# Casting k and q of the first pair inside the set-up, with its products in the score banks and one load moved to another queue

## The chip, the cores and the metric

The kernel runs on one core of one Trainium2 chip. The metric is device microseconds (us) for one execution, measured on the chip. Each timed set also has one profiled execution. In every execution the listed time is about 1.7 us longer than the span that the profile covers, so a span of 435.3 us belongs to a time of 437.0 us.

Engines are named as in the profile: PE is TensorE, PEld its weight loads, DVE is VectorE, ACT is ScalarE, POOL is GpSimd, SP is SyncE.

## The reference

Two stages follow each other. The first is causal attention with a decay that comes from a running sum of log(f). The second is a spectral mix: a Fourier transform along the sequence, one complex 512 x 512 matrix for each of 64 modes, the inverse transform, and a channel product.

```python
# batch 8, heads 8, seq 576, head_dim 64; 64 modes, d_model 512
scores = (q @ k.T) / sqrt(64) + (cum[:, None] - cum[None, :])   # cum = cumsum(log f), causal
attn   = softmax(scores);  x = attn @ v          # heads side by side: [8, 576, 512]
X = rfft(x, axis=1)[:, :64]                      # Xr, Xi
Yr = einsum('bmd,mde->bme', Xr, w_r) - einsum('bmd,mde->bme', Xi, w_i)
Yi = einsum('bmd,mde->bme', Xr, w_i) + einsum('bmd,mde->bme', Xi, w_r)
u  = x + irfft(Y, n=576);  out = u + relu(u @ w_ch)
```

The mode matrices w_r and w_i are 64 x 512 x 512 numbers of 4 bytes each, 134 MB together. They are read once and cast to bf16 on the way in.

## The kernel before

The attention runs in 32 steps. A step is one head of one pair of batches; two steps share one "pair" of loads (k, q, v). Weights are loaded into a ring of 9 tiles, and a tile comes free when the mode products that read it are done. All loads but f and the v of pair 0 are issued by GpSimd in program order.

```python
def emit_loads(pr):                       # k, q, v of one pair
    for nm, src in (("k", k), ("q", q), ("v", v)):
        ...
        if nm == "v" and pr < 1:
            nc.sync.dma_start(dst, ap)    # SP's queue
        else:
            pool_dma(dst, ap)             # GpSimd's queue, in program order
...
nc.vector.tensor_copy(ident_f[:, :], ident_bf[:, :])
...                                        # sel, memsets
nc.scalar.activation(lf[:], ft[:], ACT.Ln)
nc.vector.tensor_tensor_scan(cum[:], onesS[:], lf[:], 0.0, ALU.mult, ALU.add)
cum_ps = psT.tile([128, NSB, BH], F32, tag="tr", name="cum_ps")   # transpose banks
...                                        # transposes of cum, copies, R_ps, Rb
nc.vector.tensor_tensor(biasA[...], Rb..., cumT..., ALU.subtract)
nc.scalar.activation(wdec[:, :, :], biasA[:, :, :], ACT.Exp)
for r0, n in RG:
    cum9_ps = psT.tile([128, 5, BH], F32, tag="tr", name="cum9_ps")
    ...                                    # transposes, subtractions into bias9
nc.scalar.activation(wdec9[:, :, :, :], bias9[:, :, :, :], ACT.Exp)
...
emit_transposes(0, "kqv")   # cast k, q, v of pair 0, transpose them on PE, copy KT, QT, VT
for s in range(NS + 1):
    pr, h = s // 2, s % 2
    if s == 0:
        emit_loads(STG - 1)
    if h == 1 and pr + STG < NPR:
        emit_loads(pr + STG)
    ...                                    # early weight loads; transposes of pair pr + 1
    emit_scores(s, 0); emit_av(s - 1, [0, 1, 2]); emit_scores(s, 1); emit_scores(s, 2)
    if s > B:                              # from step 5 on
        while nmode < (s - B) * NTH // (NS - B):
            emit_modes(nmode)              # 32 or more products of one weight tile
            nmode += 1
            next_w()                       # the load that takes the freed ring tile
    emit_av(s - 1, [3, 4]); emit_scores(s, 3); emit_vback(s)
    ...                                    # step 2: the Fourier basis; even steps: emit_dft
```

Each engine's order of instructions is settled when the kernel is built, unless an instruction is pinned to its place in the program (`keep_in_program_order`).

The softmax here doesn't subtract the row's maximum and nothing guards it: scores larger than these inputs give would overflow.

Of the kernel before, what the change touches and what calls it, by code (L numbers as in the profile page):

```python
# [8 lines left out]
F32 = mybir.dt.float32  # L9
BF16 = mybir.dt.bfloat16  # L10
I32 = mybir.dt.int32
ALU = mybir.AluOpType
# [9 lines left out]
def kernel(  # L22
# [66 lines left out]

    def pool_dma(dst, src):  # L90
        tc.keep_in_program_order(nc.gpsimd.dma_start(dst, src))  # L91
# [133 lines left out]
    with ExitStack() as actx:  # L225
# [34 lines left out]
        def emit_loads(pr):  # L260
            dc, bp, _ = steps[2 * pr]
            for nm, src in (("k", k), ("q", q), ("v", v)):
# [7 lines left out]
                if nm == "v" and pr < 1:  # L270
                    nc.sync.dma_start(dst, ap)
                else:
                    pool_dma(dst, ap)

# [56 lines left out]
        nc.vector.tensor_copy(ident_f[:, :], ident_bf[:, :])  # L331
        for r, t in enumerate(sel):
            nc.vector.memset(t[:, :], 0.0)
            nc.vector.tensor_copy(
                _strided(t[:, 1:2], [[2, 64]]), _strided(ident_bf[:, r : r + 1], [[2, 64]])
            )
# [12 lines left out]
        nc.vector.tensor_tensor_scan(cum[:], onesS[:], lf[:], 0.0, ALU.mult, ALU.add)  # L349
        cum_ps = psT.tile([128, NSB, BH], F32, tag="tr", name="cum_ps")  # L350
# [8 lines left out]
        for h in range(2):  # L359
            nc.vector.tensor_copy(  # L360
                cum2[:, :, h, :], _strided(cum[:, 0:1], [[1, NR], [NR, RP]])
            )
        cumT = scratch(128, NSB, BH)
        nc.vector.tensor_copy(cumT[:, 0:4, :], cum_ps[:, 0:4, :])
        nc.vector.tensor_copy(cumT[:64, 4, :], cum_ps[:64, 4, :])
        ones_row = scratch(1, 128)
        nc.vector.memset(ones_row[:], 1.0)
        R_ps = psT.tile([128, BH], F32, tag="tr", name="R_ps")
        nc.tensor.matmul(
            R_ps[:],  # L370
# [6 lines left out]
        nc.vector.tensor_copy(Rb[:], R_ps[:])  # L377
        biasA = scratch(128, NSB, BH)
        nc.vector.tensor_tensor(
            biasA[:, 0:4, :],  # L380
            _strided(Rb[:, :], [[0, 4], [1, BH]]),
            cumT[:, 0:4, :],
            ALU.subtract,
        )
        nc.vector.tensor_tensor(
            biasA[:64, 4, :], Rb[:64, :], cumT[:64, 4, :], ALU.subtract
        )
        nc.vector.memset(biasA[64:128, 4, :], 0.0)
# [5 lines left out]
        for r0, n in RG:  # L394
            cum9_ps = psT.tile([128, 5, BH], F32, tag="tr", name="cum9_ps")
# [6 lines left out]
            for h in range(2):  # L402
                hs = slice(h * 64, h * 64 + 64)
                nc.vector.tensor_tensor(
                    bias9[hs, r0 : r0 + n, :, :],
                    _strided(Rb[hs, h : h + 1], [[0, n], [H, B], [2, NDC]]),
                    _strided(
                        cum9_ps[hs, 0, h : h + 1], [[BH, n], [H, B], [2, NDC]]
                    ),
                    ALU.subtract,  # L410
                )
# [59 lines left out]

        QT, vaugs = {}, {}

        def emit_transposes(pr, what):
            dc, bp, _ = steps[2 * pr]
            for which in what:
                st = QKVst[pr % STG][which]
                if which == "q":
                    QT[pr] = qtp.tile([128, 2, S], BF16, tag="QT", name="QTs")
                sb = qkb.tile([128, NR, 2, Dh], BF16, tag="cb", name=which + "b")  # L480
                if which != "v":
                    ins = nc.vector.tensor_copy(
                        sb[:, :, :, :].rearrange("p r b d -> p b r d"), st[:, :, :, :]
                    )
                else:
                    ins = nc.vector.tensor_tensor(
                        sb[:, :, :, :],
                        st[:, :, :, :].rearrange("p b r d -> p r b d"),
# [629 lines left out]
```

## Time and profile before

| | before |
|---|---|
| median of 3 executions | 437.05 us (436.73 to 437.52) |
| profiled execution | 438.35 us, span 436.6 us |
| DMA share, 5 to 391 us | 1.12 to 1.14, but 1.03 at 90 to 94 us |
| first scores' exponential starts | 16.63 us |
| first ring wait of GpSimd ends | 83.34 us, after 11.74 us |
| last group of mode products starts | 401.59 us |

The page of the profile cuts the span into 40 slices of 10.9 us. These three lines are the granted clock of TensorE in tenths of full speed, the busy share of the DMA engines in tenths, and what they moved.

```profile
...
PEclk9997589999867758668668698699999896998997
DMA  8999999999999999999999999999999999994697
GB/s 181 235 235 242 234 235 239 230 193 239 230 219 235 220 229 236 212 236 229 219 236 212 211 211 211 211 211 211 212 211 211 211 211 211 211 211 97 234 365 291
...
```

The transfers are at their limit from the second slice to slice 36, and the clock is at half in parts of slices 4 to 6. The table by stage says the same in numbers. Its columns are the stretch and its length in us, busy time (and instructions) of PE, PEld, DVE, ACT and POOL, then the granted clock, the DMA share and the GB/s.

```profile
...
5.00:81.00 76.00, 60.57 (x693) 41.55 (x694) 58.86 (x164) 51.08 (x76) 26.62 (x42) 0.87 1.14 233
81.00:90.00 9.00, 8.84 (x189) 7.00 (x187) 8.24 (x24) 6.95 (x11) 3.32 (x6) 1.00 1.14 236
90.00:94.00 4.00, 4.00 (x83) 3.35 (x79) 3.18 (x11) 3.46 (x7) 2.00 (x4) 1.00 1.03 169
94.00:275.00 181.00, 145.41 (x2407) 111.14 (x2405) 114.34 (x313) 93.31 (x139) 54.72 (x83) 0.76 1.13 224
275.00:391.00 116.00, 106.00 (x1489) 65.41 (x1502) 48.78 (x105) 46.22 (x80) 32.17 (x46) 0.93 1.12 211
...
```

Only the stretch of 90 to 94 us falls off, with 169 GB/s. GpSimd's timeline of before shows why. Columns: start, length, engine, line, operation, output<-input, count, and in brackets the idle time before it and what ended that.

```profile
...
70.84 0.76 POOL L91 DMA_DIRECT2D wch<-in_moe_w_ch_dram  x1 [0.40 <-DMA stv<-in_v_dram]
83.34 0.62 POOL L91 DMA_DIRECT2D wb<-in_moe_w_r_dram  x1 [11.74 <-PE vp L524]
...
87.91 0.62 POOL L91 DMA_DIRECT2D wb<-in_moe_w_r_dram  x1 [3.34 <-PE ps L552]
...
93.28 0.64 POOL L91 DMA_DIRECT2D wb<-in_moe_w_r_dram  x1 [2.00 <-PE A L186]
...
```

GpSimd stood 11.74 us because no ring tile was free, and the next tile came 4.6 us after the first. In that time the queue ran low. The last lines needed are ScalarE's in the set-up:

```profile
...
10.41 0.47 ACT L389 ACTIVATE wdec<-Yacc 128x320 bf16<-128x320 f32 x1 [4.52 <-DVE Yacc L385]
11.74 0.44 ACT L412 ACTIVATE wdec<-Yacc 128x288 bf16<-128x288 f32 x1 [0.87 <-DVE Yacc L404]
12.94 1.36 ACT L513 COPY KT<-tp 128x640 bf16<-128x640 bf16 x2 [0.76 <-PE tp L500]
16.63 1.94 ACT L559 ACTIVATE E<-ps 128x1024 bf16<-128x1024 f32 x2 [2.32 <-PE ps L552]
```

The cast of k started on VectorE at 11.68 us, KT was copied at 12.94 us, and the first scores' exponential (L559) started at 16.63 us.

### The profile page before, as it was taken

The page shows a single profiled execution, that of the slowest core. Times are in us where ns is not written, and L with a number is a line of the kernel's source. Part 1 is how long each engine was busy: PE and PEld are TensorE (multiplying, and loading weights), DVE is VectorE, ACT ScalarE, POOL GpSimd, SP SyncE. Part 2 cuts the span into 40 slices and gives each one's busy share as a digit, 9 for nine tenths or more (in the row PEclk, how much of TensorE's full clock was granted, in tenths as well). Part 3 has the DMA queues.
Part 4 walks back from the last instruction along what each step waited for, and adds up shares of the span by engine and source line. Part 5 has one row for each costly group of instructions (what it writes and reads, how often), then busy time and mean ns, then how long its engine had stood idle before and what let it go on. Part 6 is the DMA issues. An engine that isn't in the chain of part 4 may idle for free.

```text
span 436.6 us, 12199 instructions
## 1 busy us (share of the span) xinstructions
PE 356.7 (82%) x5247; PEld 244.7 (56%) x5265; DVE 263.0 (60%) x658; ACT 224.9 (52%) x340; POOL 129.3 (30%) x202
## 2 busy tenths in 40 slices
PE   2687799998887976877778796999989778898881
PEld 1454566776666655655656565666565444554440
DVE  5687778878565665555657677333333353653892
ACT  3688378776645436446355373234434342642771
POOL 8333332153233232332333222323223223200600
PEclk9997589999867758668668698699999896998997
DMA  8999999999999999999999999999999999994697
GB/s 181 235 235 242 234 235 239 230 193 239 230 219 235 220 229 236 212 236 229 219 236 212 211 211 211 211 211 211 212 211 211 211 211 211 211 211 97 234 365 291
DMA packets 50981, 97.37 MB, mean 223 GB/s; under 512 B 3792, under 2 KB 12976, under 8 KB 50928
## 3 DMA queue, kind: packets, MB, share of 16 engines
q0 software_dynamic: 46688, 86.16, 100.8%
q1 hardware_dynamic: 3920, 9.91, 6.3%
q8 instruction: 41, 0.67, 0.6%
q10 hardware_dynamic: 320, 0.52, 0.5%
q14 instruction: 12, 0.10, 0.1%
HBM read 163.73 MB, written 9.44 MB: 397 GB/s over the span
## 4 chain that ended last, share of the span: by engine, by line
PE 31%; DMA 30%; ACT 11%; DVE 10%; issue 5%; POOL 0%; DVEq 0%; ACTq 0%; SPq 0%
DMA wb<-in_moe_w_i_dram 27%; ACT E L559 7%; PE pav L597 7%; PE ps L552 6%; PE tp L500 5%; PE A L186 5%; DMA stv<-in_v_dram 3%; PE px L640 2%; DVE QTs L515 2%; PE vp L524 2%; ACT KT L513 2%; DVE XT L654 1%; DVE os L984 1%; PE pz L806 1%; DVE E L574 1%
## 5 line engine op out<-in xcount | busy, mean ns | idle before, releaser
L559 ACT ACTIVATE E<-ps 128x1024 bf16<-128x1024 f32 (+1 forms) x128 | 101.7, 855 | 23.8 <-PE ps L552 14.3
L186 PE MATMUL A<-XT,wb 128*128 128x16 bf16 x1984 | 70.7, 182 | 14.2 <-DMA wb<-in_moe_w_i_dram 9.2
L186 PEld LDWEIGHTS <-wb 128*128 128x128 bf16 x1984 | 63.8, 100 | 28.6 <-issue 11.8
L91 POOL DMA_DIRECT2D wb<-in_moe_w_r_dram x64 | 42.9, 670 | 123.5 <-DMA wb<-in_moe_w_r_dram 20.2
L552 PE MATMUL ps<-QTs,KT 64*128 64x64 bf16 (+4 forms) x384 | 55.3, 313 | 18.5 <-ACT E L559 17.2
L91 POOL DMA_DIRECT2D wb<-in_moe_w_i_dram x64 | 42.4, 663 | 83.4 <-DMA wb<-in_moe_w_i_dram 42.3
L597 PE MATMUL pav<-va,E 128*128 128x65 bf16 (+1 forms) x1088 | 53.4, 206 | 4.0 <-DVE x_all L619 3.5
L597 PEld LDWEIGHTS <-E 128*128 128x128 bf16 (+1 forms) x1088 | 43.8, 111 | 19.7 <-issue 9.5
L574 DVE TENSOR_TENSOR E<-E,trimask 128x256 bf16<-128x256 bf16 (+2 forms) x128 | 37.3, 303 | 19.8 <-ACT E L559 19.7
L517 ACT COPY VT<-tp 128x640 bf16<-128x640 bf16 (+1 forms) x32 | 23.1, 757 | 32.4 <-PE tp L500 32.3
L845 ACT CAST XW<-pxw 128x512 bf16<-128x512 f32 x36 | 20.7, 587 | 36.7 <-PE pxw L838 31.8
L888 ACT CAST XW<-pB 128x512 bf16<-128x512 f32 x36 | 20.9, 586 | 31.7 <-PE pB L806 26.3
L552 PEld LDWEIGHTS <-KT 64*128 64x128 bf16 x384 | 18.9, 97 | 30.4 <-issue 21.2
L887 DVE CAST x_all<-pA 128x512 bf16<-128x512 f32 x36 | 24.9, 692 | 17.1 <-PE pA L806 15.3
L838 PE MATMUL pxw<-wch,yy 128*128 128x512 bf16 x133 | 33.7, 386 | 1.1 <-issue 0.5
L513 ACT COPY KT<-tp 128x640 bf16<-128x640 bf16 (+1 forms) x32 | 22.1, 754 | 22.1 <-PE tp L500 22.1
L515 DVE COPY QTs<-tp 128x640 bf16<-128x640 bf16 (+1 forms) x32 | 23.3, 768 | 14.3 <-PE tp L500 14.2
L619 DVE TENSOR_TENSOR x_all<-pav,rcp 128x384 bf16<-128x384 f32 x64 | 29.1, 455 | 0.8
L151 DVE TENSOR_TENSOR YTe<-A,Yacc 128x128 bf16<-128x128 f32 x16 | 5.9, 366 | 33.2 <-PE A L186 33.2
L608 DVE RECIPROCAL rcp<-pav 128x6 f32<-128x6 f32 x64 | 12.1, 190 | 21.4 <-PE pav L597 20.7
L806 PEld LDWEIGHTS <-ident_bf 64*64 64x64 bf16 (+1 forms) x300 | 14.4, 110 | 17.1 <-issue 9.7
L500 PE MATMUL tp<-ident_bf,qb 128*128 128x128 bf16 x144 | 17.4, 276 | 4.6 <-ACT KT L513 3.9
(143 smaller groups left out, 607.9 us busy)
## 6 DMA issues: line engine op xcount, KB each, us to landing
wb<-in_moe_w_r_dram POOLq DMA_DIRECT2D x62, 512.0 KB, 16.9
wb<-in_moe_w_i_dram POOLq DMA_DIRECT2D x62, 512.0 KB, 17.8
stv<-in_v_dram POOLq DMA_DIRECT2D x10, 576.0 KB, 15.2
out_dram<-os SPq DMA_DIRECT2D x10, 512.0 KB, 5.5
stk<-in_k_dram POOLq DMA_DIRECT2D x11, 288.0 KB, 15.3
stq<-in_q_dram POOLq DMA_DIRECT2D x11, 288.0 KB, 15.3
wx<-in_v_dram POOLq DMA_DIRECT2D x5, 576.0 KB, 15.1
out_dram<-uo SPq DMA_DIRECT2D x3, 512.0 KB, 3.9
```

The source lines that it names most:

```text
L91: tc.keep_in_program_order(nc.gpsimd.dma_start(dst, src))
L186: nc.tensor.matmul(A[:, eb, mi, :], lhsT=w_of(mi, eb * 128), rhs=x_of(m), start=(i == 0), stop=(i == len(terms) - 1),)
L500: nc.tensor.transpose(tp[:, r - r0, :, :].rearrange("c h p -> c (h p)"), sb[:, r, :, :].rearrange("p b d -> p (b d)"), ident_bf[:, :],)
L513: nc.scalar.copy(rows(KTs[pr % 2][:, :, 0:S]), tv)
L515: nc.vector.tensor_copy(rows(QT[pr][:, :, :]), tv)
L552: nc.tensor.matmul(ps[:, b, o : o + n], lhsT=KTs[pr % 2][bs, h, jb * 128 : (jb + 1) * 128], rhs=QT[pr][bs, h, jb * 128 + c0 : jb * 128 + c ...
L559: nc.scalar.activation(E[:, :, piece * 512 : piece * 512 + w], ps[:, :, 0:w], ACT.Exp, scale=scale,)
L574: nc.vector.tensor_tensor(dg, dg, tr, ALU.mult)
L597: nc.tensor.matmul(pav[64 * half : 64 * half + w, slot, :], lhsT=E[:, b, c : c + (w - 1) * st + 1 : st], rhs=va[:, jb, b, :], start=(n == ...
L619: nc.vector.tensor_tensor(xo, pi, ri, ALU.mult)
L838: nc.tensor.matmul(pxw[:, :], lhsT=xT[:, eb, i * 128 : (i + 1) * 128], rhs=wch[:, eb, :], start=(eb == 0), stop=(eb == NDC - 1),)
L887: nc.vector.tensor_copy(xs, pA[:, :])
```

## The change

The change brings the first scores forward. The casts of k and q of pair 0 stand amid the set-up, the set-up's products use the score banks, so that the transpose banks are free for k and q, VectorE's order is pinned, and the v of pair 1 goes to SP's queue behind f and the v of pair 0. No arithmetic is added or removed.

```diff
-                if nm == "v" and pr < 1:
+                if nm == "v" and pr < 2:
                     nc.sync.dma_start(dst, ap)
@@ the set-up (keep = tc.keep_in_program_order)
-        nc.vector.tensor_copy(ident_f[:, :], ident_bf[:, :])
-        for r, t in enumerate(sel): ...            # now after emit_transposes(0, "v")
-        nc.vector.tensor_tensor_scan(cum[:], onesS[:], lf[:], 0.0, ALU.mult, ALU.add)
-        cum_ps = psT.tile([128, NSB, BH], F32, tag="tr", name="cum_ps")
+        keep(nc.vector.tensor_tensor_scan(cum[:], onesS[:], lf[:], 0.0, ALU.mult, ALU.add))
+        keep(nc.vector.tensor_copy(ident_f[:, :], ident_bf[:, :]))
+        cum_ps = psS.tile([128, 2, 512], F32, tag="sc", name="cum_ps")
+        cum_ps = cum_ps[:, 0, 0 : NSB * BH].rearrange("p (s c) -> p s c", s=NSB)
 ...                                                # R_ps and cum9_ps likewise to psS
+        emit_transposes(0, "k")
+        keep(nc.vector.tensor_copy(Rb[:], R_ps))
 ...                                                # the biasA subtractions, each kept
+        emit_transposes(0, "q")
         nc.scalar.activation(wdec[:, :, :], biasA[:, :, :], ACT.Exp)
 ...                                                # the bias9 subtractions, each kept
-        emit_transposes(0, "kqv")
+        emit_transposes(0, "v")
```

More of the change, by code (lines that the diff above doesn't have):

```diff
@@ L88, in tile_of @@
         return 2, g ^ 4 if GL // 2 <= g < GL else g
+    keep = tc.keep_in_program_order
     def pool_dma(dst, src):
-        tc.keep_in_program_order(nc.gpsimd.dma_start(dst, src))
+        keep(nc.gpsimd.dma_start(dst, src))
     def wb_tile(n, *dims):
@@ L273, in emit_loads, with emit_transposes, rows @@
                     pool_dma(dst, ap)
+        QT, vaugs = {}, {}
+        def emit_transposes(pr, what):
+            dc, bp, _ = steps[2 * pr]
+            for which in what:
+                st = QKVst[pr % STG][which]
+                if which == "q":
+                    QT[pr] = qtp.tile([128, 2, S], BF16, tag="QT", name="QTs")
+                sb = qkb.tile([128, NR, 2, Dh], BF16, tag="cb", name=which + "b")
+                if which != "v":
+                    ins = nc.vector.tensor_copy(
+                        sb[:, :, :, :].rearrange("p r b d -> p b r d"), st[:, :, :, :]
+                    )
+                else:
+                    ins = nc.vector.tensor_tensor(
+                        sb[:, :, :, :],
+                        st[:, :, :, :].rearrange("p b r d -> p r b d"),
+                        _strided(
+                            wdec9[:, 0, 2 * bp, dc : dc + 1],
+                            [[B * NDC, NR], [NDC, 2], [0, Dh]],
+                        ),
+                        ALU.mult,
+                    )
+                if pr < STG:
+                    tc.keep_in_program_order(ins)
+                for r0, n in RG:
+                    tp = psT.tile([128, 5, 2, RP], BF16, tag="tr", name="tp")
+                    for r in range(r0, r0 + n):
+                        nc.tensor.transpose(
+                            tp[:, r - r0, :, :].rearrange("c h p -> c (h p)"),
+                            sb[:, r, :, :].rearrange("p b d -> p (b d)"),
+                            ident_bf[:, :],
+                        )
+                    tv = tp[:, 0:n, :, :].rearrange("c r h p -> c h p r")
+                    def rows(t):
+                        return t.rearrange("c h (p r) -> c h p r", r=NR)[
+                            :, :, :, r0 : r0 + n
+                        ]
+                    if which == "k":
+                        nc.scalar.copy(rows(KTs[pr % 2][:, :, 0:S]), tv)
+                    elif which == "q":
+                        ins = nc.vector.tensor_copy(rows(QT[pr][:, :, :]), tv)
+                        if pr == 0:
+                            keep(ins)
+                    else:
+                        nc.scalar.copy(rows(VTs[pr % 2][:, :, 0:S]), tv)
         used = [0]
@@ L330 @@
         )
-        nc.vector.tensor_copy(ident_f[:, :], ident_bf[:, :])
-        for r, t in enumerate(sel):
-            nc.vector.memset(t[:, :], 0.0)
-            nc.vector.tensor_copy(
-                _strided(t[:, 1:2], [[2, 64]]), _strided(ident_bf[:, r : r + 1], [[2, 64]])
-            )
         for t in VTs:
@@ L348 @@
         cum = scratch(BH, S)
-        nc.vector.tensor_tensor_scan(cum[:], onesS[:], lf[:], 0.0, ALU.mult, ALU.add)
-        cum_ps = psT.tile([128, NSB, BH], F32, tag="tr", name="cum_ps")
+        keep(
+            nc.vector.tensor_tensor_scan(
+                cum[:], onesS[:], lf[:], 0.0, ALU.mult, ALU.add
+            )
+        )
+        keep(nc.vector.tensor_copy(ident_f[:, :], ident_bf[:, :]))
+        cum_ps = psS.tile([128, 2, 512], F32, tag="sc", name="cum_ps")
+        cum_ps = cum_ps[:, 0, 0 : NSB * BH].rearrange("p (s c) -> p s c", s=NSB)
         for sc in range(NSB):
@@ L359 @@
         for h in range(2):
-            nc.vector.tensor_copy(
-                cum2[:, :, h, :], _strided(cum[:, 0:1], [[1, NR], [NR, RP]])
+            keep(
+                nc.vector.tensor_copy(
+                    cum2[:, :, h, :], _strided(cum[:, 0:1], [[1, NR], [NR, RP]])
+                )
             )
         cumT = scratch(128, NSB, BH)
-        nc.vector.tensor_copy(cumT[:, 0:4, :], cum_ps[:, 0:4, :])
-        nc.vector.tensor_copy(cumT[:64, 4, :], cum_ps[:64, 4, :])
+        keep(nc.vector.tensor_copy(cumT[:, 0:4, :], cum_ps[:, 0:4, :]))
+        keep(nc.vector.tensor_copy(cumT[:64, 4, :], cum_ps[:64, 4, :]))
         ones_row = scratch(1, 128)
-        nc.vector.memset(ones_row[:], 1.0)
-        R_ps = psT.tile([128, BH], F32, tag="tr", name="R_ps")
+        keep(nc.vector.memset(ones_row[:], 1.0))
+        R_ps = psS.tile([128, 2, 512], F32, tag="sc", name="R_ps")[:, 0, 0:BH]
         nc.tensor.matmul(
-            R_ps[:],
+            R_ps,
             lhsT=ones_row[0:1, :],
@@ L376 @@
         Rb = ssb.tile([128, BH], F32, name="Rb")
-        nc.vector.tensor_copy(Rb[:], R_ps[:])
+        emit_transposes(0, "k")
+        keep(nc.vector.tensor_copy(Rb[:], R_ps))
         biasA = scratch(128, NSB, BH)
-        nc.vector.tensor_tensor(
-            biasA[:, 0:4, :],
-            _strided(Rb[:, :], [[0, 4], [1, BH]]),
-            cumT[:, 0:4, :],
-            ALU.subtract,
-        )
-        nc.vector.tensor_tensor(
-            biasA[:64, 4, :], Rb[:64, :], cumT[:64, 4, :], ALU.subtract
-        )
-        nc.vector.memset(biasA[64:128, 4, :], 0.0)
+        keep(
+            nc.vector.tensor_tensor(
+                biasA[:, 0:4, :],
+                _strided(Rb[:, :], [[0, 4], [1, BH]]),
+                cumT[:, 0:4, :],
+                ALU.subtract,
+            )
+        )
+        keep(
+            nc.vector.tensor_tensor(
+                biasA[:64, 4, :], Rb[:64, :], cumT[:64, 4, :], ALU.subtract
+            )
+        )
+        keep(nc.vector.memset(biasA[64:128, 4, :], 0.0))
+        emit_transposes(0, "q")
         nc.scalar.activation(wdec[:, :, :], biasA[:, :, :], ACT.Exp)
@@ L394 @@
         for r0, n in RG:
-            cum9_ps = psT.tile([128, 5, BH], F32, tag="tr", name="cum9_ps")
+            cum9_ps = psS.tile([128, 2, 512], F32, tag="sc", name="cum9_ps")
+            cum9_ps = cum9_ps[:, 0, 0 : 5 * BH].rearrange("p (r c) -> p r c", r=5)
             for r in range(r0, r0 + n):
@@ L403 @@
                 hs = slice(h * 64, h * 64 + 64)
-                nc.vector.tensor_tensor(
-                    bias9[hs, r0 : r0 + n, :, :],
-                    _strided(Rb[hs, h : h + 1], [[0, n], [H, B], [2, NDC]]),
-                    _strided(
-                        cum9_ps[hs, 0, h : h + 1], [[BH, n], [H, B], [2, NDC]]
-                    ),
-                    ALU.subtract,
+                keep(
+                    nc.vector.tensor_tensor(
+                        bias9[hs, r0 : r0 + n, :, :],
+                        _strided(Rb[hs, h : h + 1], [[0, n], [H, B], [2, NDC]]),
+                        _strided(
+                            cum9_ps[hs, 0, h : h + 1], [[BH, n], [H, B], [2, NDC]]
+                        ),
+                        ALU.subtract,
+                    )
                 )
@@ L469, in emit_basis @@
                 )
-        QT, vaugs = {}, {}
-        def emit_transposes(pr, what):
-            dc, bp, _ = steps[2 * pr]
-            for which in what:
-                st = QKVst[pr % STG][which]
-                if which == "q":
-                    QT[pr] = qtp.tile([128, 2, S], BF16, tag="QT", name="QTs")
-                sb = qkb.tile([128, NR, 2, Dh], BF16, tag="cb", name=which + "b")
-                if which != "v":
-                    ins = nc.vector.tensor_copy(
-                        sb[:, :, :, :].rearrange("p r b d -> p b r d"), st[:, :, :, :]
-                    )
-                else:
-                    ins = nc.vector.tensor_tensor(
-                        sb[:, :, :, :],
-                        st[:, :, :, :].rearrange("p b r d -> p r b d"),
-                        _strided(
-                            wdec9[:, 0, 2 * bp, dc : dc + 1],
-                            [[B * NDC, NR], [NDC, 2], [0, Dh]],
-                        ),
-                        ALU.mult,
-                    )
-                if pr < STG:
-                    tc.keep_in_program_order(ins)
-                for r0, n in RG:
-                    tp = psT.tile([128, 5, 2, RP], BF16, tag="tr", name="tp")
-                    for r in range(r0, r0 + n):
-                        nc.tensor.transpose(
-                            tp[:, r - r0, :, :].rearrange("c h p -> c (h p)"),
-                            sb[:, r, :, :].rearrange("p b d -> p (b d)"),
-                            ident_bf[:, :],
-                        )
-                    tv = tp[:, 0:n, :, :].rearrange("c r h p -> c h p r")
-                    def rows(t):
-                        return t.rearrange("c h (p r) -> c h p r", r=NR)[
-                            :, :, :, r0 : r0 + n
-                        ]
-                    if which == "k":
-                        nc.scalar.copy(rows(KTs[pr % 2][:, :, 0:S]), tv)
-                    elif which == "q":
-                        nc.vector.tensor_copy(rows(QT[pr][:, :, :]), tv)
-                    else:
-                        nc.scalar.copy(rows(VTs[pr % 2][:, :, 0:S]), tv)
         def emit_vback(s):
@@ L691, in next_w @@
                 nload += 1
-        emit_transposes(0, "kqv")
+        emit_transposes(0, "v")
+        for r, t in enumerate(sel):
+            nc.vector.memset(t[:, :], 0.0)
+            nc.vector.tensor_copy(
+                _strided(t[:, 1:2], [[2, 64]]), _strided(ident_bf[:, r : r + 1], [[2, 64]])
+            )
         for s in range(NS + 1):
```

## The prediction

> **What bounds it now.** The transfers. The 40-slice strip and the table by stage show DMA busy and flat from 2 us to 391 us: share 1.14 at 5–81 us, 1.13 at 94–275, 1.12 at 275–391 (211 GB/s written for weights cast from f32 to bf16, so about twice that read, an estimate). The Trainium skill, "DMA: Bandwidth & Descriptors" (Anatomy of one DMA), fits a transfer's variable part at 436 GB/s; 2 x 211 = 422 agrees. The chain of waits has 27% of the span on weight transfers, end to end from 275 to 395 us. Then comes a tail of about 42 us of products and output stores, which the change does not touch.
>
> Only three places are not saturated: the start (0–2 us nothing, share 0.89 at 2–5 us); a dip at 90–94 us (169 GB/s, share 1.03, lowest 0.85); the tail. The dip comes from GpSimd's issue list: after 71.6 us it stands 11.7 us because the weight ring is full, until the first mode products end at 83.3 us; the queue then runs nearly dry. Against 210 GB/s the slices of 85–95 us lost about 0.2 MB, worth 0.4 to 1.0 us (an estimate). The chain of waits confirms it: at 70–87 us it runs through ScalarE exponentials and matmuls, then through the weight issues.
>
> **What the change does.** No arithmetic is added or removed.
> - VectorE: the identity cast (0.21 us) moves ahead of the two 1.34 us copies of the sums, so TensorE's transposes of the sums start near 6.2 instead of 7.53 us. The casts of k and q (0.46, 0.45 us) fill waits for the products (0.65 us before the copy at 9.56); the five bias subtractions of the second exponential (0.65 + 0.58 us) go behind the QT copies. QT should end near 12.8 instead of 15.93 us.
> - ScalarE: the KT copies (1.36 us) now come before the Exp table load. That load (1.28 us in the trace; the same 1283 ns in "ScalarE: Activation LUTs", What ACT_TABLE_LOAD costs) was hidden at 4.60 us; now it follows KT, at about 11.3 us. Both decay exponentials precede the first scores' exponential, and the second waits for the bias subtractions, so it starts near 14.5 instead of 16.63 us. vb starts near 14.6 instead of 15.83 us.
> - Set-up products in the score banks free the transpose banks.
> - v of pair 1 moves from GpSimd's queue (0.73 us of issuing) to SP's: same bytes, same 16 engines.
>
> So attention runs 1 to 2 us earlier. Through pair 3 loads lie several us ahead of their casts (pair 2's k lands about 24.5, is cast at 29.1), so the shift should survive to 83 us. There it can only close the dip at 90–94 us. From there the transfers are saturated again, and earlier compute merely waits.
>
> **Prediction.** Gain 0.7 us of the dip, 0 to 0.3 at the start: 436.2 us (range 434.4 to 437.7). Faster by over 2%: 0.02; within 2%: 0.96; slower by over 2%: 0.02.
>
> **What would show it.** First scores' exponential near 14.5 us; GpSimd's long wait ends 1–2 us before 83.3 us; the 90–94 us dip shallower; last weight issue (385.45 us before) and end of transfers 0.5–1 us earlier; 211 GB/s at 275–391 unchanged; tail unchanged.
>
> **What would make it wrong.** TensorE's granted clock drops to 0.50 in stretches (38–58 us); a shift could move one into the tail or the 70–83 us stretch, plus or minus 1–2 us. v of pair 1 beside k and q of pair 0 may delay their landing and eat the shift. If the queue's waits, not bandwidth, set the flat 211 GB/s, more than 1 us could be won.

## The result, and the profile after

Ratios here are the mean time of one kernel's fast executions over that of the other's of the same rounds, so they are not quite the ratio of the medians quoted beside them.

| | before | after |
|---|---|---|
| median | 437.28 us (436.73 to 437.52, 4 executions) | 437.75 us (437.36 to 438.0, 4 executions) |
| ratio | 1 | 1.0012, 95% interval 0.9994 to 1.0029: the same |
| profiled execution | span 436.6 us | span 436.2 us |

The predicted gain of 0.8 us did not come. The median is 0.05 us above the predicted range. The trace of the changed kernel nevertheless shows much of what was expected. The table by stage of after:

```profile
...
5.00:81.00 76.00, 59.35 (x685) 39.35 (x685) 58.78 (x167) 50.72 (x75) 25.51 (x41) 0.91 1.14 232
81.00:90.00 9.00, 8.83 (x165) 6.65 (x164) 6.97 (x18) 6.71 (x10) 2.39 (x4) 1.00 1.15 233
90.00:94.00 4.00, 4.00 (x87) 3.28 (x88) 3.12 (x12) 2.85 (x5) 3.46 (x6) 1.00 1.12 206
94.00:275.00 181.00, 150.28 (x2377) 113.98 (x2375) 114.62 (x315) 94.11 (x141) 54.31 (x81) 0.71 1.13 223
275.00:391.00 116.00, 105.14 (x1501) 65.17 (x1518) 50.07 (x108) 46.39 (x81) 32.14 (x46) 0.93 1.12 211
...
```

The dip at 90 to 94 us is nearly gone, 206 instead of 169 GB/s (a shorter one stands earlier: the slices of 85 to 87 us have 174 and 172 GB/s, in before 185 and 199), and 275 to 391 us is unchanged at 211 GB/s. The set-up on ScalarE in after:

```profile
...
10.74 1.36 ACT L318 COPY KT<-tp 128x640 bf16<-128x640 bf16 x2 [6.37 <-PE tp L305]
12.12 1.28 ACT L448 ACT_TABLE_LOAD   x1
13.42 0.47 ACT L448 ACTIVATE wdec<-Yacc 128x320 bf16<-128x320 f32 x1
15.75 0.44 ACT L474 ACTIVATE wdec<-Yacc 128x288 bf16<-128x288 f32 x1 [1.86 <-DVE Yacc L465]
16.10 2.83 ACT L574 ACTIVATE E<-ps 128x1024 bf16<-128x1024 f32 x3
```

KT is copied at 10.74 instead of 12.94 us, but the first exponential of the scores starts at 16.10 us. The activation table load of 1.28 us (1283 ns in the Trainium skill, "ScalarE: Activation LUTs", What ACT_TABLE_LOAD costs), which was hidden before, is now in the row, and the second decay exponential waits 1.86 us for VectorE. VectorE's timeline of after shows the beginning of that chain:

```profile
...
9.47 0.46 DVE L287 COPY kb<-stk 128x1152 bf16<-128x1152 bf16 x1 [1.52 <-DMA stk<-in_k_dram]
...
11.03 0.46 DVE L287 COPY qb<-stq 128x1152 bf16<-128x1152 bf16 x1 [0.22 <-DMA stq<-in_q_dram]
12.65 1.55 DVE L320 COPY QTs<-tp 128x640 bf16<-128x640 bf16 x2 [1.16 <-PE tp L305]
...
```

The cast of k waited 1.52 us for its own data (stk), and the first copy of QT started at 12.65 us. And GpSimd's first ring wait did not end earlier:

```profile
...
71.64 0.76 POOL L93 DMA_DIRECT2D wch<-in_moe_w_ch_dram  x1 [0.39 <-DMA stv<-in_v_dram]
83.73 0.61 POOL L93 DMA_DIRECT2D wb<-in_moe_w_r_dram  x1 [11.32 <-PE pav L612]
...
88.84 0.61 POOL L93 DMA_DIRECT2D wb<-in_moe_w_r_dram  x1 [3.89 <-PE ps L567]
...
92.18 0.67 POOL L93 DMA_DIRECT2D wb<-in_moe_w_r_dram  x1
...
```

It ended at 83.73 us, against 83.34 us. So of a lead of 0.5 us at the first exponential nothing was left at 83 us. Two traces of one execution each cannot tell which of this belongs to the kernels.

### The profile page after: what moved, and what is told of

The parts are those of the page before. It is cut to its first block, busy times and chain, and to the rows that moved or that the text cites. A ratio compares the mean times of both kernels' runs of the same rounds, so it can differ in the third digit from the quotient of the medians.

```text
span 436.2 us, 12199 instructions
## 1 busy us (share of the span) xinstructions
PE 359.0 (82%) x5247; PEld 245.1 (56%) x5265; DVE 263.1 (60%) x658; ACT 224.9 (52%) x340; POOL 128.2 (29%) x201
## 4 chain that ended last, share of the span: by engine, by line
DMA 40%; PE 28%; ACT 8%; DVE 6%; issue 4%; POOL 1%; DVEq 0%; ACTq 0%; SPq 0%; POOLq 0%
DMA wb<-in_moe_w_i_dram 39%; PE pav L612 7%; PE ps L567 6%; ACT E L574 6%; PE tp L305 5%; PE A L188 5%; DVE QTs L320 2%; ACT KT L318 1%; PE vp L539 1%; DVE os L1004 1%; PE px L655 1%; PE px L680 1%; ACT VT L324 1%; DVE E L589 1%; POOL yy L821 1%
## 5 line engine op out<-in xcount | busy, mean ns | idle before, releaser
L574 ACT ACTIVATE E<-ps 128x1024 bf16<-128x1024 f32 (+1 forms) x128 | 101.4, 849 | 24.8 <-PE ps L567 14.5
L188 PE MATMUL A<-XT,wb 128*128 128x16 bf16 x1984 | 69.5, 181 | 13.2 <-DMA wb<-in_moe_w_i_dram 9.0
L567 PE MATMUL ps<-QTs,KT 64*128 64x64 bf16 (+4 forms) x384 | 59.5, 324 | 20.6 <-ACT E L574 18.6
L612 PE MATMUL pav<-va,E 128*128 128x65 bf16 (+1 forms) x1088 | 55.5, 210 | 2.7 <-DVE x_all L634 2.3
L612 PEld LDWEIGHTS <-E 128*128 128x128 bf16 (+1 forms) x1088 | 45.6, 114 | 18.0 <-issue 9.1
L567 PEld LDWEIGHTS <-KT 64*128 64x128 bf16 x384 | 20.0, 99 | 36.2 <-issue 24.6
L655 PE MATMUL px<-bas,x_all 128*128 128x128 bf16 x160 | 18.8, 270 | 2.4 <-ACT XT L673 1.8
```

Source lines behind the costliest of these rows:

```text
L188: nc.tensor.matmul(A[:, eb, mi, :], lhsT=w_of(mi, eb * 128), rhs=x_of(m), start=(i == 0), stop=(i == len(terms) - 1),)
L567: nc.tensor.matmul(ps[:, b, o : o + n], lhsT=KTs[pr % 2][bs, h, jb * 128 : (jb + 1) * 128], rhs=QT[pr][bs, h, jb * 128 + c0 : jb * 128 + c ...
L574: nc.scalar.activation(E[:, :, piece * 512 : piece * 512 + w], ps[:, :, 0:w], ACT.Exp, scale=scale,)
L612: nc.tensor.matmul(pav[64 * half : 64 * half + w, slot, :], lhsT=E[:, b, c : c + (w - 1) * st + 1 : st], rhs=va[:, jb, b, :], start=(n == ...
```

## The experiments

Theory A: the set-up's time is passed on through the ring wait and the transfers to the end, but less of it arrives than predicted. Theory B: some slack, or the tail, swallows it. Within A, parts of the change may hurt: the v of pair 1 on SP may hold up the k of pair 0 and change the order on the engines. In all there were 18 runs, several of them of the same kernel. "Lead" below is the amount of data landed at 384 us, less that of the first trace of before, summed from tables by stage of 2 us (good to about 0.02 MB). At 211 GB/s, 0.1 MB is 0.47 us.

### Both kernels again, and the load moved alone

before_again is before unchanged, after_again is the changed kernel unchanged. after_vpool undoes one part of the change, before_vsp does that part alone:

```diff
# after_vpool, from after             # before_vsp, from before
-  if nm == "v" and pr < 2:           -  if nm == "v" and pr < 1:
+  if nm == "v" and pr < 1:           +  if nm == "v" and pr < 2:
```

Expected of before_again:

> The kernel before, unchanged, to learn what one trace is worth. Theory 'floor' (transfers set the time; only the dip near 90 us can be won): ratio 1.000 within 0.15%; the new trace again has GpSimd's long wait for a weight ring tile ending at 83.3 plus or minus 0.3 us, and again a stretch of two or more 1 us slices under 190 GB/s between 85 and 95 us. Rival 'noise' (the dip that the prediction counted on is a chance of one execution): the wait ends elsewhere by over 0.5 us, or the dip is absent or half as deep.

Expected of after_again:

> The changed kernel, unchanged, with five rounds to settle the sign. Theory 'floor': ratio 0.998 to 1.001; first scores' exponential at 16.1 us, the long ring wait ends at 83.7, about 0.1 MB more landed than in the kernel before from 94 us on, the last weight lands 0.2 to 0.5 us earlier. Rival 'slower in truth' (the median of 4 runs was 0.5 us up): ratio 1.001 to 1.002 with an interval above 1, and the trace shows a later landing of the last weight or a longer tail.

Expected of after_vpool:

> The changed kernel with v of pair 1 back on GpSimd's queue. Theory 'v on SP ate the lead': k of pair 0 lands before 8.6 us and its cast does not wait (9.47 us and 1.52 us of waiting in the changed kernel), first scores' exponential at 14.3 to 15.0 us; the 64-wide score piece stays ahead of the sine table load, so the lead survives 35 to 43 us and the long ring wait ends at 81.5 to 82.5 us; the dip closes; with 'floor' the ratio is 0.997 to 0.999 (0.4 to 1.2 us). Rival 'set-up on the path one to one': about 2 us faster, 0.995. Rival 'v on SP is harmless': k lands as in the changed kernel and nothing moves.

Expected of before_vsp:

> The kernel before with v of pair 1 on SP alone. Theory 'v on SP ate the lead': k of pair 0 lands after 9.0 us, here without harm since its cast comes at 11.7; GpSimd's issues of pairs 2 and 3 come 0.4 to 0.8 us later; the order near the sine tables changes, and the long ring wait ends 0.5 to 1.5 us later than 83.3. Ratio 0.999 to 1.003. Rival: no change in any of these marks.

Measured, 5 rounds, one chip; the shared executions of before gave 437.48 us (436.61 to 438.89, 11 of them):

| | median us | ratio (95%) | k cast | first exp. | ring wait ends | lead MB |
|---|---|---|---|---|---|---|
| before_again | 437.15 | 0.9995 (0.9975 to 1.0014) | 11.52 | 16.47 | 83.54 | -0.02 |
| after_again | 437.46 | 0.9999 (0.9980 to 1.0019) | 7.93 | 14.98 | 82.52 | +0.20 |
| after_vpool | 437.55 | 0.9997 (0.9978 to 1.0015) | 7.82 | 15.08 | 80.93 | +0.18 |
| before_vsp | 440.87 | 1.0082 (1.0044 to 1.0120) | 11.52 | 16.55 | 85.40 | -0.22 |

The changed kernel's cast of k started at 7.93 us here after a gap of only 0.14 us, so the length of the 1.52 us wait of the first trace was a feature of that execution. In after_vpool the cast did not wait and the ring wait ended earlier, as expected, but the time did not fall to the expected 0.997 to 0.999. The load of v alone made the kernel before 0.8% slower, where 0.999 to 1.003 had been expected. And single executions of one unchanged kernel scatter by more than 2 us, which is more than the whole predicted gain.

### A dose in the bad direction

after_late runs the set-up's scan three times instead of once. The order on VectorE, ScalarE, GpSimd and SP is otherwise that of after.

```diff
-        keep(nc.vector.tensor_tensor_scan(cum[:], onesS[:], lf[:], 0.0, ALU.mult, ALU.add))
+        for _ in range(3):
+            keep(nc.vector.tensor_tensor_scan(cum[:], onesS[:], lf[:], 0.0, ALU.mult, ALU.add))
```

> A dose in the bad direction: the changed kernel with the set-up's scan run three times instead of once on VectorE (the same values written again; no other instruction moves on any engine). One scan is about 1.3 us in the traces, so the first scores' exponential should come about 2.5 us later, at 17.5 to 18.5 us instead of 15.0 to 16.1. Theory A (the set-up time is passed on to the end, and a gain of under 1 us merely drowns in the scatter of single executions): GpSimd's long ring wait ends about 2.5 us later (85 to 86 us), the dip after 84 us is back, at 390 us the transfers are 0.3 to 0.5 MB behind the changed kernel's (1.5 to 2.5 us at 211 GB/s), and the time is 438.7 to 440, ratio to before 1.003 to 1.006. Theory B (slack before the first mode takes up the set-up time): ring wait ends under 1 us later, transfers level, time 437.0 to 437.8, ratio 0.999 to 1.001.

The three scans took 4.12 us. The first exponential came at 17.97 us and the first ring wait ended at 84.93 us, 1.2 to 2.4 us later than in the five traces of the changed kernel. The lead was -0.05 MB, 0.13 to 0.25 MB less than there. The median was 438.52 us beside 438.23 us of before (ratio 1.0017, 0.9989 to 1.0046). The delay is therefore passed on to the ring and to the transfers, as theory A has it, but the ring wait moved by less than 2.7 us and the transfers by less than the expected 0.3 to 0.5 MB. The time alone decides nothing.

### Taking the dip away without touching the set-up

before_modes puts the first two groups of mode products at the end of step 4. after_vm does the same to after_vpool.

```diff
                 if h == 0:
                     emit_dft(pr - 1)
+            if s == B:
+                while nmode < 2:
+                    emit_modes(nmode)
+                    nmode += 1
+                    next_w()
```

> The dip is taken away without touching the set-up: the kernel before, with the first two groups of modes put right after the first transform (at the end of step 4) instead of inside step 5, so that the second ring tile comes free about 3 us earlier. Expected in the trace: the first ring wait ends as in before (about 83.4 us), the second weight tile is issued at about 85 instead of 88 us, the slices from 86 us on are at 200 GB/s or more, at 390 us the transfers are 0.1 to 0.2 MB ahead of before (0.5 to 0.9 us). If the closed dip is worth what the traces say, the median is 436.5 to 437.0 (ratio 0.998 to 0.999); if something after 390 us takes it back, 437.2 to 437.8 although the transfers lead.

> Both together: after_vpool with the first two groups of modes at the end of step 4. If the dip is all that the weights' stream can win, this adds nothing to after_vpool, since no dip is left there (transfers 0.2 MB ahead of before at 390 us, time within 0.3 us of after_vpool2). If freeing the ring earlier wins more than the dip, transfers lead by 0.3 MB or more and the time is 436.2 or less.

Both were slower: before_modes 442.51 us (ratio 1.0115, 1.0090 to 1.0140), after_vm 440.70 us (1.0067, 1.0044 to 1.0090). The edit was badly made. The two weight loads moved ahead of the loads of pair 5 and of wch in GpSimd's order, and GpSimd stood still before them, as its timeline in before_modes shows:

```profile
...
63.46 0.62 POOL L91 DMA_DIRECT2D wb<-in_moe_w_i_dram  x1 [1.82 <-DMA wb<-in_moe_w_r_dram]
82.19 0.61 POOL L91 DMA_DIRECT2D wb<-in_moe_w_r_dram  x1 [18.11 <-PE tp L500]
...
```

It was blocked for 18.11 us, the transfers stopped, and at 384 us the traces were 0.88 and 0.66 MB behind. That is a usable calibration all the same. At 211 GB/s these are 4.2 and 3.1 us, and the mean times were 4.9 and 2.8 us above before. So a lag in the transfers reaches the end nearly whole.

before_modes2 is the repaired edit: the products stand early, the loads stay where they were. after_vm2 is the same edit of after_vpool.

```diff
+            if s == B:
+                for n in range(2):
+                    emit_modes(n)
...
-                    emit_modes(nmode)
+                    if nmode >= 2:
+                        emit_modes(nmode)
                     nmode += 1
                     next_w()
```

> The dip taken away in the kernel before, this time without moving any transfer: the first two groups of modes stand at the end of step 4 as in before_modes, but the loads of weights stay where they were, so that GpSimd issues all transfers in the order of before (before_modes had put two of them ahead of the loads of pair 5, blocked GpSimd from 64 to 82 us and lost 0.88 MB). Expected: second weight tile issued at 85 to 86 us instead of 88, dip gone from 87 us on, at 390 us 0.1 to 0.2 MB ahead of before, and, if a lead is passed on as before_modes and after_vm show a lag to be (0.88 MB and 0.66 MB behind cost 4 and 3 us), a ratio of 0.998 to 0.999 (436.5 to 437.0). If the end takes leads of under 1 us back, 0.9995 to 1.0005.

GpSimd's timeline in before_modes2 shows the second ring tile (84.16 us) right behind the first, where before had 87.91 us:

```profile
...
82.28 0.61 POOL L91 DMA_DIRECT2D wb<-in_moe_w_r_dram  x1 [10.97 <-PE tp L500]
...
84.16 0.61 POOL L91 DMA_DIRECT2D wb<-in_moe_w_r_dram  x1 [0.64 <-PE tp L500]
...
```

No slice of 1 us from 84 to 96 us is under 200 GB/s, and the lead is 0.20 MB, as expected. The profiled execution took 436.37 us, 0.8 us under the mean of before on that chip. But the six executions lay between 436.33 and 439.01 us, median 437.95 us, ratio 1.0013 (0.9993 to 1.0034). The dip can be closed without touching the set-up. What it is worth does not show above the scatter.

### More executions

> The same kernel as after_vpool once more (the changed kernel with the v of pair 1 back on GpSimd's queue), for more executions. The trace should again show no dip (first ring wait ending near 81 us, all slices from 84 us at 190 GB/s or more) and transfers about 0.2 MB ahead of before at 390 us. If that lead is worth its 0.9 us, the median of the fast runs is 436.4 to 436.9; if the lead is lost at the end, 437.2 to 437.7.

> The changed kernel once more, for more executions and one more look at when the k of pair 0 lands. Passed on: half to all of the 0.10 to 0.21 MB lead, ratio to before 0.998 to 0.999. Taken back: 0.9995 to 1.0005. If the landing of k varies with the v of pair 1 ahead of it on the other queue, the cast of k starts anywhere between 7.9 and 9.5 us.

> after_vpool a third time, for more executions: its two looks lead by 0.18 to 0.23 MB at 390 us, its two medians have ratios of 0.9997 and 0.9996. A lead passed on would be 0.998; taken back, 0.9995 to 1.0005.

> The kernel before with the v of pair 1 on SP, once more: its first run was 0.8% slower (437.1 us span in the profile, but 438 to 444 in the other executions), more than the 0.22 MB that its profile was behind explain (1 us). If its cost is real and varies with the execution, the ratio is again 1.005 to 1.012 and this profile shows another depth of the dip after 85 us; if the first run was a fluke of that chip, the ratio is 1.001 to 1.004.

| | median us | ratio (95%) | k cast | ring wait ends | lead MB | span of the trace |
|---|---|---|---|---|---|---|
| after_vpool2 | 437.38 | 0.9996 (0.9970 to 1.0022) | 7.94 | 82.39 | +0.23 | 436.5 |
| after_again2 | 438.01 | 1.0023 (1.0007 to 1.0039) | 8.59 | 82.86 | +0.16 | 434.8 |
| after_vpool3 | 437.26 | 1.0004 (0.9988 to 1.0020) | 7.82 | 80.74 | +0.24 | 436.5 |
| before_vsp2 | 440.28 | 1.0084 (1.0053 to 1.0116) | 11.47 | 86.11 | -0.35 | 438.3 |

The cost of before_vsp is real: two chips gave 1.0082 and 1.0084. In its traces the cast of k and the first exponential stand where before has them (16.55 and 16.42 us), so the landing of k is not the reason there. The ring wait ends at 85.40 and 86.11 us, 2.5 and 3.2 us later than in before on average. The line is from GpSimd's timeline of before_vsp2, with columns as above:

```profile
...
86.11 0.62 POOL L91 DMA_DIRECT2D wb<-in_moe_w_r_dram  x1 [14.45 <-PE vp L524]
...
```

After_vpool, with the same load back on GpSimd's queue, has its ring wait end at 79.9 to 82.4 us in four traces, and its cast of k always at 7.8 to 7.9 us without a wait. The lines are from VectorE's and then GpSimd's timeline of after_vpool3:

```profile
...
7.82 0.38 DVE L287 COPY kb<-stk 128x1152 bf16<-128x1152 bf16 x1
...
```

```profile
...
80.74 0.61 POOL L93 DMA_DIRECT2D wb<-in_moe_w_r_dram  x1 [8.69 <-PE vp L539]
...
```

Yet its times were no better. That was the open question for the last runs.

### Where a lead goes

> The kernel before, unchanged. Theory 1 (half clock over the last weights decides): a trace without it at 396 to 400 us has its last group of modes waiting for a weight transfer and a span of 435.0 to 435.5 us; a trace with it has no such wait and a span of 436.3 to 436.8. Theory 2 and 3 (set-up or drain): the span does not depend on where the half clock falls. The cast of k starts at 11.5 to 11.7 us in either.

> The changed kernel, unchanged. Theory 1: without half clock at 396 to 400 us a span of 434.7 to 435.6 us, with it 436.0 to 436.5. Theory 2: the cast of k starts between 7.9 and 10 us, the first exponential follows it by about 6.7 us, and the lead at 390 us falls by about 0.1 MB per 1 us of it. Theory 3: the drain after VectorE's last result is longer than the 8.5 us of before. The ratio of the times is 0.9995 to 1.002.

> As before_x2; its timed executions, with those of before_x2 and of the shared runs, give the scatter of one kernel on one chip (standard deviation 0.7 to 1.0 us expected).

> As after_x3. Taken with after_x3 the mean of the timed executions is within 0.5 us of that of the three sets of before.

All four ran on one chip. The shared executions of before gave 438.16 us (436.12 to 439.06); the ratios are 1.0001 (0.9975 to 1.0027) and 1.0014 (0.9983 to 1.0045) for before_x2 and before_x3, 1.0020 (0.9991 to 1.0048) and 1.0021 (0.9996 to 1.0047) for after_x3 and after_x4. The traces separate cleanly. For each, the stretch of 396 to 400 us of the table by stage (clock, share and GB/s last), then the last group of mode products on TensorE's timeline. First before_x2, span 435.3 us:

```profile
...
396.00:400.00 4.00, 3.12 (x56) 1.62 (x52) 1.30 (x3) 1.17 (x2) 0.00 (x0) 1.00 0.47 95
...
```

```profile
...
399.74 0.36 PE L170 MATMUL A<-XT,wb 128*128 128x16 bf16 x8 [0.59 <-DMA wb<-in_moe_w_i_dram]
...
```

before_x3, span 437.2 us:

```profile
...
396.00:400.00 4.00, 4.00 (x46) 1.85 (x43) 1.26 (x3) 0.69 (x2) 0.00 (x0) 0.58 0.63 124
...
```

```profile
...
401.95 0.36 PE L170 MATMUL A<-XT,wb 128*128 128x16 bf16 x8
...
```

after_x3, span 435.1 us:

```profile
...
396.00:400.00 4.00, 3.33 (x58) 1.73 (x54) 1.51 (x3) 1.17 (x2) 0.00 (x0) 1.00 0.48 97
...
```

```profile
...
399.79 0.36 PE L172 MATMUL A<-XT,wb 128*128 128x16 bf16 x8 [0.31 <-DMA wb<-in_moe_w_i_dram]
...
```

after_x4, span 437.1 us:

```profile
...
396.00:400.00 4.00, 4.00 (x51) 2.07 (x49) 1.31 (x3) 0.75 (x2) 0.00 (x0) 0.60 0.56 112
...
```

```profile
...
401.89 0.36 PE L172 MATMUL A<-XT,wb 128*128 128x16 bf16 x8
...
```

Where the clock is full over the last weights (1.00), the last group waits for its data and starts at 399.7 to 399.8 us. Where it is at half for most of the stretch (0.58, 0.60), TensorE is busy all 4.00 us, the last group waits for nothing, and it starts at 401.9 us. Of the difference of about 2 us between the two executions of one kernel, part is the lead (before_x2 0.27 and before_x3 -0.07 MB; after_x3 0.20 and after_x4 0.08 MB) and the rest goes with the clock. The two spans with half clock are 0.4 and 0.6 us above what had been expected.

The last two runs asked whether this clock belongs to after_vpool.

> after_vpool a fourth time. If the half clock over the last weights falls by chance, this trace has it with a chance of about one half; without it the last group of modes waits for its weights and the span is 434.5 to 435.2 us (time 436.2 to 436.9), with it 436.2 to 436.6 (437.9 to 438.3). If it belongs to this kernel, the trace has it. The timed executions fall into two clusters 1 to 2 us apart, ratio 0.9985 to 1.0005.

> after_vpool with the first two groups of modes at the end of step 4 and all transfers in the order of after_vpool (the repaired after_vm). No dip in the trace, second weight tile issued 1.5 to 2 us after the first, transfers 0.2 to 0.3 MB ahead of before at 390 us; since after_vpool has no dip left, no more than 0.05 MB more than after_vpool. Time: within 0.5 us of after_vpool4, ratio 0.998 to 1.001.

after_vpool3, span 436.5 us, and after_vpool4, span 434.3 us, are the same kernel:

```profile
...
396.00:400.00 4.00, 3.77 (x40) 1.69 (x36) 1.67 (x4) 1.17 (x2) 0.00 (x0) 0.57 0.48 98
...
```

```profile
...
400.99 0.36 PE L172 MATMUL A<-XT,wb 128*128 128x16 bf16 x8
...
```

```profile
...
396.00:400.00 4.00, 3.24 (x60) 1.69 (x56) 1.43 (x3) 1.17 (x2) 0.00 (x0) 1.00 0.46 95
...
```

```profile
...
399.69 0.36 PE L172 MATMUL A<-XT,wb 128*128 128x16 bf16 x8 [0.49 <-DMA wb<-in_moe_w_i_dram]
...
```

The half clock is not tied to the kernel. Without it, after_vpool gave the fastest execution, 436.04 us. The six executions of this set lie in two clusters, 436.04 and 436.72, and four of 438.31 to 438.72 us, so that the median is 438.35 us (ratio 1.0024, 1.0004 to 1.0043). after_vm2 had the half clock, a lead of 0.18 MB, and 437.71 us (1.0016, 1.0000 to 1.0032). Neither beats before, and both ratios are above the expected ones.

### All traces together

| trace | first exp. | first x_all | ring wait ends | from x_all | lead MB | half clock over the last weights | span |
|---|---|---|---|---|---|---|---|
| before | 16.63 | 26.22 | 83.34 | 57.1 | 0 | yes | 436.6 |
| before_again | 16.47 | 26.98 | 83.54 | 56.6 | -0.02 | no | 435.4 |
| before_x2 | 16.47 | 26.01 | 81.27 | 55.3 | +0.27 | no | 435.3 |
| before_x3 | 16.57 | 26.28 | 83.62 | 57.3 | -0.07 | yes | 437.2 |
| after | 16.10 | 25.73 | 83.73 | 58.0 | +0.10 | no | 436.2 |
| after_again | 14.98 | 24.57 | 82.52 | 58.0 | +0.20 | no | 435.6 |
| after_again2 | 15.24 | 24.97 | 82.86 | 57.9 | +0.16 | no | 434.8 |
| after_x3 | 15.05 | 24.76 | 82.65 | 57.9 | +0.20 | no | 435.1 |
| after_x4 | 15.64 | 25.27 | 83.26 | 58.0 | +0.08 | yes | 437.1 |
| after_vpool | 15.08 | 24.40 | 80.93 | 56.5 | +0.18 | yes | 436.3 |
| after_vpool2 | 15.20 | 24.52 | 82.39 | 57.9 | +0.23 | yes | 436.5 |
| after_vpool3 | 15.07 | 24.39 | 80.74 | 56.4 | +0.24 | yes | 436.5 |
| after_vpool4 | 15.19 | 24.59 | 79.87 | 55.3 | +0.24 | no | 434.3 |

(x_all is the attention's output; "from x_all" is the time from its first write to the end of the first ring wait.)

A straight-line fit through all 20 traces, the slowed ones included, gives (the table leaves out the seven of the kernels with extra work or moved parts; of these after_late, after_vm2, before_vsp2 and the two blocked kernels, whose last weights came later, count as having half clock over the last weights): span = 435.8 us - 3.7 us for each MB of lead + 1.3 us if the clock is at half over the last weights. The standard errors are 0.35 us per MB and 0.2 us. Without the two blocked kernels it is 3.4 with an error of 0.7, and again 1.3 us. This is a fit, not an experiment on the clock, which nothing here could switch. It leaves a scatter of 0.45 us.

## Why the prediction was right or wrong

**What bounds the kernel: right.** The two blocked kernels show it best. 0.88 and 0.66 MB behind in the transfers cost 4.9 and 2.8 us. The transfer rate that the prediction took from the Trainium skill, "DMA: Bandwidth & Descriptors" (Anatomy of one DMA), 436 GB/s, also agrees with every trace: 211 GB/s written as bf16 from f32 are 422 GB/s read.

**The first scores' exponential at 14.5 us: too early by 0.5 to 1.6 us.** Five traces have 14.98 to 16.10 us. Two terms were missed. The cast of k waits for its data in four of the five traces (by 0.57 to 1.52 us; it starts at 7.9 to 9.5 us), with the v of pair 1 moving on the other queue at that time; with that v on GpSimd's queue (after_vpool) it starts at 7.8 to 7.9 us every time, without a wait. The prediction named this danger and put no time on it. And in after the bias subtractions behind the QT copies ended only at 15.65 us, with the second decay exponential waiting 1.86 us for them; they had been costed, but QT ended at 14.20 us, not 12.8.

**"So the shift should survive to 83 us": this is the step that failed.** The attention's first output comes at 25.1 us on average in the five traces of the changed kernel and at 26.4 us in the four of before, so the shift is there and is 1.3 us. From that output to the end of the first ring wait the changed kernel takes 57.9 to 58.0 us in every trace (after_late, which has that load on SP too, 57.3 us), before 55.3 to 57.3 us, on average 56.6 us. The ring wait ends at 83.0 and 82.9 us: the shift has gone. Taking back the v of pair 1 (after_vpool) brings that time to 56.5 us on average (55.3 to 57.9) and the ring wait to 81.0 us. So the loss is caused by the v of pair 1 on SP. The first output, from VectorE's timelines of before and then of after, whose ring waits are shown above:

```profile
...
26.22 0.56 DVE L619 TENSOR_TENSOR x_all<-pav,rcp 128x384 bf16<-128x384 f32 x1
...
```

```profile
...
25.73 0.55 DVE L634 TENSOR_TENSOR x_all<-pav,rcp 128x384 bf16<-128x384 f32 x1
...
```

It does not come through the landing of k, since it is counted from 25 us on, and since before_vsp loses 2 us there with its k cast on time. Nor is it the clock. Half clock between 35 and 60 us does go with a longer time here: before has 57.1 and 57.3 us with 20.5 us of it, 56.6 and 55.3 us with 13.7, and after_vpool2 its 57.9 us with 20.5. But the changed kernel has only 13.7 to 17.1 us of it, and before_vsp, with 20.5, takes 58.4 and 58.9 us.

The traces show where the time goes. From the first exponential of step 3 to that of step 5 the changed kernel takes 21.8 to 22.3 us, after_vpool 20.2 to 21.1, before 21.2 to 21.4 and before_vsp 23.6. Moving the load changes the built order there. In after_again and after_vpool step 3 starts at 30.97 us. ScalarE's timeline of after_again, then of after_vpool:

```profile
...
34.41 1.28 ACT L512 ACT_TABLE_LOAD   x1
...
37.98 1.19 ACT L574 ACTIVATE E<-ps 128x128 bf16<-128x128 f32 x2
40.43 1.02 ACT L574 ACTIVATE E<-ps 128x1024 bf16<-128x1024 f32 x1 [1.25 <-PE ps L567]
...
```

```profile
...
30.97 3.02 ACT L574 ACTIVATE E<-ps 128x1024 bf16<-128x1024 f32 x4 [0.65 <-PE pav L612]
34.01 1.28 ACT L512 ACT_TABLE_LOAD   x1
...
```

With the v on SP the last of step 3's four exponentials (128x128) stands behind the two activation table loads around the sines of the Fourier basis, and the next one waits 1.25 us for its scores; with the v on GpSimd's queue all four come first, as the expectation of after_vpool had said. before has the second order and before_vsp the first, and in this stretch no TensorE, VectorE or ScalarE instruction waits for a DMA in any of these traces. The order was not changed by itself, so it is the path that the traces show, not one that an experiment isolates.

This step explains the lost lead, but not by itself the missing gain: in after_vpool the shift does survive, with a lead of 0.22 MB on average, and its times are still no lower than those of before.

**The worth of the dip, 0.7 us: mis-sized.** It was read from one trace. Before has that dip in some executions and hardly in others: before_x2 ends its ring wait at 81.27 us, has no dip and is 0.27 MB ahead. On average the changed kernel leads before by 0.10 MB at 384 us (0.15 less 0.045), which the fit turns into 0.4 us, where the prediction had 0.7 us.

**211 GB/s at 275 to 391 us unchanged: right. The dip at 90 to 94 us shallower: right in the trace** (206 against 169 GB/s), and it occurs in before as well. **The last weight issue earlier: wrong in the first trace** (385.95 against 385.45 us). On average of the five and four traces it comes 0.1 us earlier (384.9 against 385.0 us), where 0.5 to 1 us had been predicted.

**The tail unchanged: wrong in one term.** Its work is the same, but an execution with half granted clock over the last weights is 1.3 us longer by the fit, in either kernel. The prediction named this risk as plus or minus 1 to 2 us, and a range of 434.4 to 437.7 us did not leave it enough room.

**The base.** The 437.05 us were the median of three executions. The sets of before timed later have medians of 437.48, 438.23, 437.48, 438.16 and 437.07 us. A change with no effect at all would have missed the range in some of these sets.

**What stays open.** Over all chips, 24 executions of the changed kernel in the later sets are 0.5 us (plus or minus 0.35, 95%, the error of before's own mean left out) above before on the same chip, although its five traces have a shorter mean span than before's four (435.8 and 436.1 us). The 24 of after_vpool are 0.1 us above (plus or minus 0.4), although it leads in all its traces by what the fit would turn into 0.7 us over before: what takes this back was not found, and half clock over the last weights in three of its four traces is a guess. Whether the half clock falls on the last weights more often in these kernels, four traces of one kernel cannot say. And before_vsp is 3.5 us slower on average in 12 executions, up to 444 us, while its two profiled ones (438.84 and 440.01 us) are only 1.2 and 2.9 us above the mean of before on their chips, of which their lag in the transfers makes 0.8 and 1.3 us by the fit. What happened in the others was not seen.

## What to carry to other kernels

When the expected gain is below the scatter of single executions, take several traces of the kernel before, and read the size of a loss from all of them before calling it winnable. A lead in the set-up counts only at the point where the bound resource waits for it: compare the time from the lead to that point in both kernels, since one moved load can use it up. When several parts go in together, undo each part alone; here the part that looked free (a load on an idle queue) was the one that cost.

## What the Trainium skill lacked or had wrong

- "TensorE: Matmul & The Clock Gate" (What's actually happening) gives half rate as the state after an idle window of about 3.4 us and says that the window is free-running. A free-running window would agree with one kernel being seen with and without half clock over its last weights. But in before_x3 TensorE is busy all 4.00 us of 396 to 400 us at a mean clock of 0.58, and the last idle time before that was 1.93 us, for a weight transfer. In all 20 traces there are also 10.2 to 20.5 us of half clock between 35 and 60 us, in before with TensorE busy 17.45 of 21 us, and the longest idle time of TensorE from 26 to 44 us is 0.92 us there. Half clock without an idle window of 3.4 us is not covered by that section. The page's section "A second HAM failure mode: psum-queue depth-cycling" tells of another kernel that swings between half and full rate because TensorE idles shortly and often, but gives no length of idle time at which this begins.
- "DMA: Bandwidth & Descriptors" (Queues, rings and completion order) says that each DMA engine takes turns between the queues that it has work for. The traces agree, but the section does not say what such a load costs another that is waited for. Here, with 0.59 MB of v on the second queue, the cast of k started at 7.9 to 9.5 us in five traces, without it at 7.8 to 8.1 us in the six of after_vpool, after_vm and after_vm2.
- I found no page that says how far single executions of one kernel scatter. Here 23 of before on one chip lie between 436.12 and 439.84 us.
